# Chunked attention and a gated feed-forward layer on one Trainium2 core: GpSimd's sums of weights handed out seven in five steps instead of two a step

## The chip, the core and the metric

The kernel runs on one core of one Trainium2 chip. The metric is the device time of the whole program in microseconds (us): the median of several runs.

## The reference

Attention works within chunks of 64 positions (8 batches, 8 heads, 576 positions, 64 values per head), and its output, as 4608 tokens of 512 numbers, goes through a gated layer with 1536 inner columns:

```python
scores = scale * np.matmul(q_c, k_c.transpose(0, 1, 2, 4, 3))      # per chunk of 64
scores = scores - np.max(scores, axis=-1, keepdims=True)
attn = np.exp(scores)
attn = attn / (np.sum(attn, axis=-1, keepdims=True) + 1e-09)
out = np.matmul(attn, v_c)
x = out.transpose(0, 2, 1, 3).reshape(B * S, H * D)                # 4608 x 512
gate = 1.0 / (1.0 + np.exp(-(x @ w_gate)))                          # 512 x 1536
val = x @ w_val
return gate * val @ w_out                                           # 1536 x 512
```

## The kernel before

The tokens are nine blocks m of 512. Weights come in twelve groups f of 128 inner columns. All matmul operands are split into a high and a low part, and three products of the parts make one exact enough product (`up`, line 253; `down`, line 281).

**Blocks 0 to 2** run one step per group f: `step(m, f)` (line 602) issues the gate and value products g (12 + 12 matmuls, line 261), ScalarE's sigmoid (`hf`, line 270), VectorE's gating (line 272) and the split into `hh` (ScalarE, line 274) and `hl` (VectorE, line 276); `finish()` then adds the output products of the step before to the four accumulators `acc` (line 287). So "step (2,1)" means block 2, group 1, and the output products of (1,11) stand behind the g products of (2,0). The first two steps of block 1 run earlier; `rest()` (line 645) begins with step (1,2). At the last group, `evacuate` (line 294) copies the four accumulators, even ones on VectorE (line 307), odd ones on ScalarE (line 305), into `ob` and sends them out (line 308).

**Blocks 3 to 8** run in three pairs with a scheme that needs seven products in place of eight, for which it needs sums and differences of weights. These are made once, during blocks 1 and 2, and kept in DRAM: there are 24 **units** (6 pairs of groups, gate or value, 2 halves). `keep_sums` (line 331) makes one unit: on GpSimd (POOL in the profile) two additions of weights into `a_val` (line 338), four 128x128 additions and subtractions into `a_sum` (line 344), and the split into `a_both` (lines 346 and 347); then SyncE issues one 512 KB store of it to `sums` (line 348). `a_val` and `a_sum` take the two buffers of the tag "ob", which `evacuate` of blocks 0 and 1 uses for `ob` too; `a_both` has one buffer. `keep_given` and `keep_outer` copy other weights to DRAM and need no engine but SyncE's queue.

**Attention** of the later blocks is worked in between: `flow()` (line 506) gives pieces. A piece S has the score products `sc` of two units of heads (line 170) and asks for the next queries and keys (`load`, line 144: `qt`, `kbd`, two buffers each); a piece A has the value products `av` (line 231) and asks for the next values (`load_values`, line 155: `vt`). The rest of it is VectorE and ScalarE work that `tick` deals out.

**What sets the order.** On TensorE from the stage `MIDDLE` on, and on VectorE in `rest()`, instructions stand in the order in which the code issues them. ScalarE, GpSimd and SyncE are put in order by the framework's scheduler. Buffers are handed round in the order of the code: an `ob` of block 1 asked for after twenty units has to wait for the twentieth unit's reads. All transfers are issued from one queue, SyncE's (SP, SPq in the profile), and its instructions go one after the other: a transfer that has to wait for data holds every transfer behind it.

`keep(n)` (line 637) takes up to n units from the list; `rest()` calls `keep(2)` behind each step and its `finish()` (line 661).

Of the kernel before, what the change touches and what calls it, by code (L numbers as in the profile page):

```python
# [48 lines left out]
def chunk_attn_moe(ctx: ExitStack, tc: tile.TileContext, q, k, v, w, out):  # L49
# [270 lines left out]
    def keep_given(p, which):  # L320

        t = given[p, which] = dp.tile([P, 3, 2, 256], F32, name=f"given{p}{which}")
        for n, (f, k) in enumerate(((2 * p, 0), (2 * p, 1), (2 * p + 1, 1))):
            nc.sync.dma_start(t[:, n], wt[f, which][:, :, k * 256:(k + 1) * 256].bitcast(F32))

    def keep_outer(f):
        if f % 2 == 0:
            outer[f // 2] = dp.tile([P, 2, 1024], F32, name=f"outer{f // 2}")
        nc.sync.dma_start(outer[f // 2][:, f % 2], wt[f, 2].rearrange("p a n -> p (a n)").bitcast(F32))

    def keep_sums(p, which, c):

        if c == 0:
            sums[p, which] = dp.tile([P, 4, 2, 256], F32, name=f"sums{p}{which}")
        val = mp.tile([P, 4, P], F32, tag="ob", name="a_val")
        for n in range(2):
            parts = wt[2 * p + n, which].rearrange("p a (k c n) -> p a k c n", k=2, c=2)[:, :, :, c].bitcast(F32)
            nc.gpsimd.tensor_tensor(out=val[:, 2 * n:2 * n + 2], in0=parts[:, 0], in1=parts[:, 1], op=ALU.add)  # L338
        sm4 = mp.tile([P, 4, P], F32, tag="ob", name="a_sum")
        for o, x, y, op in (  # L340
            (sm4[:, 1], val[:, 2], val[:, 3], ALU.add), (sm4[:, 0], sm4[:, 1], val[:, 0], ALU.subtract),
            (sm4[:, 2], val[:, 0], val[:, 2], ALU.subtract), (sm4[:, 3], val[:, 1], sm4[:, 0], ALU.subtract),
        ):
            nc.gpsimd.tensor_tensor(out=o, in0=x, in1=y, op=op)  # L344
        both = wp.tile([P, 4, 2, P], F32R, tag="spare", name="a_both")
        nc.gpsimd.tensor_copy(both[:, :, 0], sm4)  # L346
        nc.gpsimd.tensor_tensor(out=both[:, :, 1], in0=sm4, in1=both[:, :, 0].bitcast(F32), op=ALU.subtract)  # L347
        nc.sync.dma_start(
            sums[p, which][:, :, c], both.rearrange("p s a n -> p s (a n)").bitcast(F32))
# [10 lines left out]
    def load_group(n, p, which):  # L360

        one, two = place(2048), place(1536)
        for t, g, s in ((one, 2, slice(0, 2)), (two, 1, slice(2, 4))):
            g0 = 0 if g == 2 else 2
            nc.sync.dma_start(
                t[:, :g * 512].rearrange("p (g n) -> p g n", g=g).bitcast(F32),
                given[p, which][:, g0:g0 + g].rearrange("p g a n -> p g (a n)"))
            nc.sync.dma_start(
                t[:, g * 512:].rearrange("p (s n) -> p s n", s=2).bitcast(F32),
                sums[p, which][:, s].rearrange("p s c n -> p s (c n)"))  # L370
        def of_given(t, n):
            return lambda a, c: t[:, n * 512 + a * 256 + c * P:n * 512 + a * 256 + (c + 1) * P]
        def of_sums(t, n):
            return lambda a, c: t[:, n * 512 + c * 256 + a * P:n * 512 + c * 256 + (a + 1) * P]
        groups[n, p, which] = {
            1: (of_given(one, 0), "B11"), 2: (of_given(one, 1), "B21"), 6: (of_sums(one, 2), "T2"),
            5: (of_sums(one, 3), "T1"), 4: (of_given(two, 0), "T4"), 7: (of_sums(two, 1), "T3"),
            3: (of_sums(two, 2), "B22")}
# [47 lines left out]
    def sole(n, p, which):  # L426
        z = ps_g.tile([P, TB], F32, tag=f"g{which}", name="cz", bufs=1)
        product(n, p, which, 5, z, True, True)
        return z
# [143 lines left out]
    def tick(share):  # L573
        now["ticks"] += 1
        now["credit"] += share
        while now["item"] is not None:
            if isinstance(now["item"], float):
                if now["credit"] < now["item"] / 2:
                    return
                now["credit"] -= now["item"]  # L580
            elif not (now["item"] == "wait" and now["ticks"] > now["since"] + 1
                      or now["item"][0] == "open" and now["item"][1] <= now["open"]):
                break
            advance()
        now["credit"] = min(now["credit"], share)

    def insert(upto=4 * NB, pieces=0):


        if now["item"] == "S" or (  # L590
                now["item"] == "A" and now["unit"] < upto and now["ticks"] >= now["since"] + pieces):
            advance()

    def due(n):

        while now["item"] is not None and len([x for x in xc if x[0] == n]) < 7:
            advance()
# [4 lines left out]
    def step(m, f, span):  # L602
        pending.append(hidden(m, f, spans[span]))

    def finish():
        down(*pending.pop(0))
# [27 lines left out]
        run(op)  # L634
    kept = [(p, which, c) for p in range(6) for which in range(2) for c in range(2)]

    def keep(n):
        for _ in range(n):
            if kept:
                p, which, c = kept.pop(0)  # L640
                if c == 0:
                    keep_given(p, which)
                keep_sums(p, which, c)

    def rest():
        for m in range(1, FIRST_PAIR):
            upto = 4 * (m + 2) if m == 1 else 4 * (m + 3)
            for f in range(2 if m == 1 else 0, NF):
                if m == 2 and f == 7:
                    now["open"] = 0  # L650
                step(m, f, "")
                tick(SHARES[m])
                insert(upto, 2)
                finish()
                tick(SHARES[m])
                insert(upto, 2)
                if m == 1:
                    keep_outer(f)
                    if f == 11:
                        keep_outer(0), keep_outer(1)  # L660
                keep(2)
                if m == 2:
                    if f == 8:
                        for which in range(2):
                            load_group(0, 0, which)
        for n in range(3):
            m0 = FIRST_PAIR + 2 * n
            upto = 4 * (m0 + 4)
            order = [(p, which) for p in range(6) for which in range(2)]
            due(n)  # L670
            for i, (p, which) in enumerate(order):
                if i + 1 < len(order) and i > 0:
                    load_group(n, *order[i + 1])
                if pending:
                    banks[n, "z"] = sole(n, p, which)
                    while pending:
                        finish()
                first(n, p, which)
                tick(SHARES["up"])
                if i:  # L680
                    last(n, *order[i - 1])
                    tick(SHARES["up"] if i < 11 else 0)
                    insert(upto, 1)
                middle(n, p, which)
                tick(SHARES["up"] if i < 11 else 0)
                insert(upto, 1)
            load_outer(0), load_outer(1)
            parts = split(n, 0, 0)
            last(n, *order[-1])
            now["open"] = n + 1  # L690
            for b in range(2):
                for f in range(NF):
                    if f % 2 == 0:
                        later = 6 * b + f // 2 + 2
                        if later < 12:
                            load_outer(later % 6)
                        elif n + 1 < 3:
                            load_group(n + 1, 0, later - 12)
                    hh, hl = parts if f == 0 else split(n, f, b)
                    if (b, f) != (0, 0):  # L700
                        tick(SHARES["down"])
                    if (b, f) == (0, NF - 1):
                        parts = split(n, 0, 1)
                    if (n, b) == (2, 1) and f >= NF - 2:
                        pending.append((f, hh, hl))
                        continue
                    for t in range(4):
                        outward(m0 + b, f, t, hh, hl)
                    insert(upto, 1)

        for i, tiles in ((0, (0, 1, 2)), (1, (0,)), (0, (3,)), (1, (1, 2, 3))):
            f, hh, hl = pending[i]
            for t in tiles:
                outward(NB - 1, f, t, hh, hl)
# [34 lines left out]
```

## Time and profile before

| | |
|---|---|
| median of 3 runs | 956.03 us (954.69 to 957.15) |
| the profiled execution, its own time | 960.18 us |
| its span in the trace | 958.4 us |
| mean granted TensorE clock | 0.989 of full speed |
| TensorE (PE) busy | 929.6 us, 97% of the span |
| VectorE (DVE) busy | 601.8 us, 63% |
| ScalarE (ACT) busy | 340.7 us, 36% |
| GpSimd (POOL) busy | 134.1 us, 14% |

Busy times are shares of the whole span; what a stretch is limited by has to be read in that stretch. A matmul's end in the trace is modelled, so starts are the safer numbers. In square brackets behind a row of a timeline stands how long the engine had been idle before it, and what ended that.

### The profile page before, as it was taken

What the parts mean: (1) busy time and instruction counts of PE and PEld (TensorE: products, weight loads), DVE (VectorE), ACT (ScalarE), POOL (GpSimd) and SP (SyncE); (2) the same over time, 40 slices, a digit from 0 to 9 for tenths busy, and PEclk for the clock granted to TensorE, in tenths of its full rate; (3) what the DMA queues carried; (4) which work ended last, traced back from release to release, by engine and by line L of the source; (5) the groups of instructions that cost most, each with busy time, mean ns of one, the idle gap of its engine ahead of it and who ended that gap; (6) DMA issues with size and microseconds to landing.
All of it is one profiled execution on the core that took longest, in us unless ns stands there. A gap on an engine that the chain in (4) does not pass through costs nothing.

```text
span 958.4 us, 13077 instructions
## 1 busy us (share of the span) xinstructions
PE 929.6 (97%) x4960; PEld 763.5 (80%) x4960; DVE 601.8 (63%) x999; ACT 340.7 (36%) x556; POOL 134.1 (14%) x204
## 2 busy tenths in 40 slices
PE   6999999999969999999999999999999999999998
PEld 4777888888847888788888888888888888888886
DVE  6889973676527657777677675677776635544432
ACT  5799752233214323231333432313143321112222
POOL 1000006999838000000000000000000000000000
PEclk7999999999989999999999999999999999999999
DMA  8688985444453343657666756666565655556661
GB/s 270 215 287 299 307 309 180 132 133 129 136 164 109 102 132 132 193 198 226 207 212 239 252 198 218 228 202 206 179 231 191 218 211 192 196 188 209 220 220 44
DMA packets 81279, 189.61 MB, mean 198 GB/s; under 512 B 7488, under 2 KB 38208, under 8 KB 76608
## 3 DMA queue, kind: packets, MB, share of 16 engines
q1 hardware_dynamic: 81216, 188.77, 58.9%
q8 instruction: 39, 0.64, 0.3%
q14 instruction: 24, 0.20, 0.1%
HBM read 150.99 MB, written 37.75 MB: 197 GB/s over the span
## 4 chain that ended last, share of the span: by engine, by line
PE 70%; POOL 9%; DMA 8%; DVE 5%; ACT 4%; issue 2%; SPq 1%; ACTq 0%; DVEq 0%; POOLq 0%
PE acc L499 21%; PE cy L421 15%; PE cz L421 10%; PE cx L421 10%; PE g L261 6%; PE acc L287 4%; DMA w_raw<-w_in 3%; POOL a_sum L344 3%; POOL a_both L347 3%; DMA sums<-a_both 2%; POOL a_val L338 2%; PE sc L170 2%; PE av L231 2%; POOL a_both L346 1%; DMA out<-ob 1%
## 5 line engine op out<-in xcount | busy, mean ns | idle before, releaser
L261 PE MATMUL g<-xt,w 128*128 128x512 f32 (+1 forms) x960 | 208.7, 372 | 6.0 <-ACT hf L270 1.7
L261 PEld LDWEIGHTS g<-xt,w 128*128 128x128 f32 x960 | 168.1, 189 | 41.5 <-ACT hf L270 4.0
L499 PE MATMUL acc<-wr,hh 128*128 128x512 f32 x576 | 177.7, 390 | 0.0
L421 PE MATMUL cy<-xc,wr 128*128 128x512 f32 x648 | 159.4, 389 | 0.4 <-DVE u L458 0.4
L421 PEld LDWEIGHTS cy<-xc,wr 128*128 128x128 f32 x648 | 121.6, 188 | 26.0 <-DVE u L458 0.8
L499 PEld LDWEIGHTS acc<-wr,hh 128*128 128x128 f32 x576 | 107.9, 188 | 22.7 <-ACT raw L242 0.3
L499 PE MATMUL acc<-wr,hl 128*128 128x512 f32 x288 | 112.0, 389 | 0.0
L421 PE MATMUL cz<-xc,wr 128*128 128x512 f32 x432 | 106.3, 391 | 0.0
L421 PE MATMUL cx<-xc,wr 128*128 128x512 f32 x432 | 106.2, 391 | 0.0
L563 DVE STREAM_TRANSPOSE pbd<-pr 32x256 f32<-32x256 f32 x224 | 97.7, 436 | 4.1
L491 DVE TENSOR_TENSOR hl<-hid,hh 128x512 fp32r<-128x512 f32 x72 | 49.6, 688 | 79.0 <-ACT hh L489 75.8
L421 PEld LDWEIGHTS cz<-xc,wr 128*128 128x128 f32 x432 | 80.6, 188 | 17.6 <-issue 1.2
L421 PEld LDWEIGHTS cx<-xc,wr 128*128 128x128 f32 x432 | 80.7, 188 | 17.4 <-issue 0.9
L287 PE MATMUL acc<-w,hh 128*128 128x512 f32 x288 | 90.6, 396 | 1.1 <-ACT hh L274 0.7
L489 ACT CAST hh<-hid 128x512 fp32r<-128x512 f32 x72 | 44.8, 623 | 123.7 <-PE acc L499 96.3
L287 PEld LDWEIGHTS acc<-w,hh 128*128 128x128 f32 x288 | 52.6, 188 | 13.8 <-issue 1.9
L499 PEld LDWEIGHTS acc<-wr,hl 128*128 128x128 f32 x288 | 54.1, 188 | 11.3
L272 DVE TENSOR_TENSOR hf<-g,hf 128x512 f32<-128x512 f32 (+1 forms) x40 | 25.4, 635 | 57.8 <-PE g L261 53.8
L439 DVE TENSOR_TENSOR u<-cy,s 128x512 f32<-128x512 f32 x36 | 24.8, 688 | 57.9 <-PE cy L421 57.8
L338 POOL TENSOR_TENSOR a_val<-w 128x256 f32<-128x256 f32 x48 | 37.7, 805 | 163.8 <-ACT xt L249 147.4
L458 DVE TENSOR_TENSOR u<-cy,s 128x512 f32<-128x512 f32 x36 | 24.9, 690 | 53.9 <-PE cy L421 53.8
L287 PE MATMUL acc<-w,hl 128*128 128x512 f32 x144 | 56.1, 390 | 0.0
(103 smaller groups left out, 1006.5 us busy)
## 6 DMA issues: line engine op xcount, KB each, us to landing
wr<-sums SPq DMA_DIRECT2D x72, 512.0 KB, 4.5
wr<-outer SPq DMA_DIRECT2D x36, 1024.0 KB, 4.8
w_raw<-w_in SPq DMA_DIRECT2D x36, 512.0 KB, 5.8
wr<-given SPq DMA_DIRECT2D x36, 512.0 KB, 3.6
sums<-a_both SPq DMA_DIRECT2D x24, 512.0 KB, 3.5
qt<-q_in SPq DMA_DIRECT2D x36, 256.0 KB, 4.4
kbd<-k_in SPq DMA_DIRECT2D x72, 128.0 KB, 4.4
vt<-v_in SPq DMA_DIRECT2D x36, 256.0 KB, 4.1
```

Source lines behind the costliest of these rows:

```text
L261: nc.tensor.matmul(ps[:, tok], lhsT=wt[f, which][:, wpart, c:c + P], rhs=x[:, part, i, tok], start=n == 0, stop=n == 11)
L272: nc.vector.tensor_tensor(out=hf, in0=pv, in1=hf, op=ALU.mult)
L287: nc.tensor.matmul(acc[m, t], lhsT=hx[:, ts], rhs=wt[f, 2][:, wpart], start=f == 0 and i == 0, stop=f == NF - 1 and i == 2,)
L338: nc.gpsimd.tensor_tensor(out=val[:, 2 * n:2 * n + 2], in0=parts[:, 0], in1=parts[:, 1], op=ALU.add)
L344: nc.gpsimd.tensor_tensor(out=o, in0=x, in1=y, op=op)
L347: nc.gpsimd.tensor_tensor(out=both[:, :, 1], in0=sm4, in1=both[:, :, 0].bitcast(F32), op=ALU.subtract)
L421: nc.tensor.matmul(bank, lhsT=lhs(wpart, c), rhs=x[:, part, c], start=start and k == 0, stop=stop and k == 5, skip_group_check=True)
L458: nc.vector.tensor_tensor(out=u3, in0=y, in1=s1, op=ALU.add)
L489: nc.scalar.copy(hh, h)
L491: nc.vector.tensor_tensor(out=hl, in0=h, in1=hh.bitcast(F32), op=ALU.subtract)
L499: nc.tensor.matmul(acc[m, t], lhsT=hx[:, ts], rhs=wo[f][:, wpart], start=f == 0 and i == 0, stop=f == NF - 1 and i == 2)
L563: nc.vector.transpose(out=pb[dst, :, c, h, i, :], in_=ps[src, h::2, k, :])
```

## The change

`keep` no longer takes a fixed number but fills up to a total: behind step (m, f) of `rest()` the units handed out so far are to be the whole part of 7·(12m + f − 13)/5.

```diff
-    def keep(n):
-        for _ in range(n):
+    def keep(done, wanted):
+        for _ in range(wanted - done):
             if kept:
                 p, which, c = kept.pop(0)
                 if c == 0:
...
-                keep(2)
+
+                keep(24 - len(kept), (7 * (12 * m + f - 13)) // 5)
```

Counted out, with the total behind each step:

| step | (1,2) | (1,3) | (1,4) | (1,5) | (1,6) | (1,7) | (1,8) | (1,9) | (1,10) | (1,11) | (2,0) | (2,1) | (2,2) to (2,7) |
|---|---|---|---|---|---|---|---|---|---|---|---|---|---|
| before | 2 | 4 | 6 | 8 | 10 | 12 | 14 | 16 | 18 | 20 | 22 | 24 | 24 |
| changed | 1 | 2 | 4 | 5 | 7 | 8 | 9 | 11 | 12 | 14 | 15 | 16 | 18, 19, 21, 22, 23, 24 |

The evacuation of block 1 is issued by the `finish()` of step (2,0), ahead of that step's `keep`: behind 20 units before, behind 14 in the changed kernel.

The instructions of TensorE and of VectorE stand in the same order in both kernels. Three places of SyncE's queue show what moves.

**SyncE's queue ahead of block 1's four outputs** (`sums` the units' stores, `qt` and `kbd` queries and keys for a piece S, `vt` values for a piece A, `out` the evacuation). Before:

```order
L348 DMA sums_2428<-a_both 512x1x256 x2
L348 DMA sums_2537<-a_both 512x1x256
L158 DMA vt<-v_in 128x512 x2
L348 DMA sums_2537<-a_both 512x1x256
L348 DMA sums_2627<-a_both 512x1x256 x2
L149 DMA qt<-q_in 128x512
L152 DMA kbd_87<-k_in 64x2x256 x2
L149 DMA qt<-q_in 128x512
L152 DMA kbd_88<-k_in 64x2x256 x2
L158 DMA vt<-v_in 128x512 x2
L308 DMA out<-ob 128x512 x4
```

Changed:

```order
L348 DMA sums_2540<-a_both 512x1x256 x2
L149 DMA qt<-q_in 128x512
L152 DMA kbd_87<-k_in 64x2x256 x2
L149 DMA qt<-q_in 128x512
L152 DMA kbd_88<-k_in 64x2x256 x2
L158 DMA vt<-v_in 128x512 x2
L149 DMA qt<-q_in 128x512
L152 DMA kbd_87<-k_in 64x2x256 x2
L149 DMA qt<-q_in 128x512
L152 DMA kbd_88<-k_in 64x2x256 x2
L158 DMA vt<-v_in 128x512 x2
L308 DMA out<-ob 128x512 x4
```

The six stores of units 15 to 20 are gone from here. The queries and keys that stand last ahead of the outputs now have no store between them and the queries and keys before them.

**SyncE's queue behind those outputs**, up to the first load of weights for the paired blocks (`wr`). Before:

```order
L348 DMA sums_2752<-a_both 512x1x256
L152 DMA kbd_88<-k_in 64x2x256
L348 DMA sums_2869<-a_both 512x1x256 x2
L158 DMA vt<-v_in 128x512 x2
L149 DMA qt<-q_in 128x512
L152 DMA kbd_87<-k_in 64x2x256 x2
L149 DMA qt<-q_in 128x512
L152 DMA kbd_88<-k_in 64x2x256 x2
L158 DMA vt<-v_in 128x512 x2
L365 DMA wr<-given_1914 128x1024
```

Changed:

```order
L348 DMA sums_2831<-a_both 512x1x256 x2
L158 DMA vt<-v_in 128x512 x2
L348 DMA sums_2942<-a_both 512x1x256 x2
L149 DMA qt<-q_in 128x512
L152 DMA kbd_87<-k_in 64x2x256 x2
L149 DMA qt<-q_in 128x512
L152 DMA kbd_88<-k_in 64x2x256 x2
L348 DMA sums_3055<-a_both 512x1x256 x2
L348 DMA sums_3215<-a_both 512x1x256 x2
L158 DMA vt<-v_in 128x512 x2
L365 DMA wr<-given_1972 128x1024
```

Ten stores stand behind the outputs in place of four. Ahead of the rows shown, unit 15's store now stands ahead of the first keys behind the outputs, as unit 21's did before; the queries and keys shown wait behind unit 20's, and the last values shown behind unit 24's.

**SyncE's queue while the last weights are loaded** (`w_raw` from the input, `given` and `outer` copies of converted weights to DRAM, with the buffers' numbers). Before:

```order
L324 DMA given30_2312<-w_824 128x2x256
L108 DMA w_raw_1198<-w_in 128x1024
L324 DMA given30_2312<-w_824 128x2x256
L324 DMA given30_2312<-w_837 128x2x256
L329 DMA outer4_2310<-w_1180 128x1024
L324 DMA given31_2424<-w_824 128x2x256 x2
L324 DMA given31_2424<-w_837 128x2x256
L329 DMA outer5_2531<-w_1189 128x1024
L108 DMA w_raw_1317<-w_in 128x1024
```

Changed:

```order
L329 DMA outer4_2252<-w_1180 128x1024
L108 DMA w_raw_1198<-w_in 128x1024
L329 DMA outer5_2461<-w_1189 128x1024
L329 DMA outer0_2533<-w_240 128x1024
L329 DMA outer0_2533<-w_397 128x1024
L324 DMA given30_2536<-w_824 128x2x256 x2
L108 DMA w_raw_1317<-w_in 128x1024
```

The copies to DRAM are mixed anew among the loads of weights; one 512 KB copy (`outer4_2252<-w_1180`) now goes ahead of `w_raw_1198` in place of one of 256 KB. On ScalarE, one CAST of a weight moves behind a sigmoid at the same time of the program.

## Rows read from the trace of the kernel before

**Rows 1.** The page, busy tenths in 40 slices of 24 us: TensorE and GpSimd
```profile
PE   6999999999969999999999999999999999999998
...
POOL 1000006999838000000000000000000000000000
```

**Rows 2.** TensorE's timeline: start us, us, line, products, [idle before <-releaser]
```profile
263.49 5.60 PE L261 MATMUL g<-xt,w 128*128 128x512 f32 x24
277.19 1.97 PE L170 MATMUL sc<-kbd,qt 128*64 128x128 f32 x16 [8.10 <-DMA kbd<-k_in]
...
290.06 3.06 PE L261 MATMUL g<-xt,w 128*128 128x512 f32 x12 [1.30 <-DVE hf L272]
...
306.36 5.60 PE L261 MATMUL g<-xt,w 128*128 128x512 f32 x24
```

**Rows 3.** SyncE's queue, timeline around the evacuation of block 1
```profile
258.30 12.81 SPq L348 DMA_DIRECT2D sums<-a_both  x3
271.20 0.58 SPq L149 DMA_DIRECT2D qt<-q_in  x1
...
276.53 7.59 SPq L308 DMA_DIRECT2D out<-ob  x4
```

**Rows 4.** GpSimd's timeline: first unit, end of the 14th, of the 20th, start of the 21st
```profile
152.05 1.45 POOL L338 TENSOR_TENSOR a_val<-w 128x256 f32<-128x256 f32 x2 [147.36 <-ACT xt L249]
...
233.75 1.29 POOL L347 TENSOR_TENSOR a_both<-a_sum,a_both 128x512 fp32r<-128x512 f32 x1
...
269.31 1.26 POOL L347 TENSOR_TENSOR a_both<-a_sum,a_both 128x512 fp32r<-128x512 f32 x1
285.46 1.96 POOL L338 TENSOR_TENSOR a_val<-w 128x256 f32<-128x256 f32 x2 [14.89 <-DMA out<-ob]
```

**Rows 5.** VectorE's timeline: the two evacuation copies of block 1 and step (2,1)'s gating
```profile
267.25 0.69 DVE L307 COPY ob<-acc 128x512 f32<-128x512 f32 x1 [5.70 <-POOL a_sum L344]
282.55 0.69 DVE L307 COPY ob<-acc 128x512 f32<-128x512 f32 x1 [14.62 <-DMA out<-ob]
...
289.31 0.69 DVE L272 TENSOR_TENSOR hf<-g,hf 128x512 f32<-128x512 f32 x1
```

**Rows 6.** Stretches: length, busy PE PEld DVE ACT POOL (instructions), PE clock, DMA share, GB/s
```profile
277.00:281.00 4.00, 3.47 (x30) 3.13 (x32) 0.00 (x0) 0.00 (x0) 0.00 (x0) 0.50 0.84 235
...
230.00:255.00 25.00, 25.00 (x157) 20.75 (x157) 15.74 (x29) 5.80 (x9) 23.58 (x36) 1.00 0.44 143
...
96.00:130.00 34.00, 33.82 (x171) 27.20 (x170) 30.22 (x53) 22.15 (x39) 0.00 (x0) 1.00 0.92 314
```

**Rows 7.** The chain that ended last, pieces of block 2: start us, us, what
```profile
313.86 2.94 PE acc L287 x12
...
322.24 2.72 PE acc L287 x12
324.96 5.44 PE g L261 x24
330.40 1.90 PE av L231 x32
...
340.68 1.90 PE sc L170 x32
...
359.12 1.90 PE av L231 x32
```

**Rows 8.** Outputs and keys: one piece of the chain, and median us from issue to landing
```profile
276.53 5.90 DMA out<-ob
...
kbd<-k_in SPq DMA_DIRECT2D x72, 128.0 KB, 4.4
...
out<-ob SPq DMA_DIRECT2D x24, 256.0 KB, 2.2
```

**Rows 9.** VectorE's split hl, groups by form: 155 to 270 us, then 310 to 380 us
```profile
L276 DVE TENSOR_TENSOR hl<-hf,hh 128x512 fp32r<-128x512 f32 x11 | 10.2, 926 | 7.6 <-ACT hh L274 7.6
...
L276 DVE TENSOR_TENSOR hl<-hf,hh 128x512 fp32r<-128x512 f32 x8 | 5.5, 692 | 5.5 <-ACT hh L274 5.5
```

## The prediction

> **What bounds the kernel now.** I read the page's busy slices first. TensorE is at 9 tenths or more nearly everywhere; behind the first slice there is one low digit, the 6 of the twelfth slice (264 to 288 us), and that is where GpSimd falls from 8 to 3 [rows 1]. Next comes TensorE's timeline across that slice: step (2,1)'s g products start at 263.49, and the score products behind them start only at 277.19, after 8.10 us of idle that the keys' transfer ended. A second, smaller wait of 1.30 us stands ahead of the value products at 290.06, ended by VectorE's gating [rows 2].
>
> SyncE's queue tells why the keys were late. From 258.30 on it spends 12.81 us on three stores, each waiting for its unit; the queries and keys stand behind them and go out from 271.20 on, the outputs of block 1 from 276.53 [rows 3]. GpSimd tells why the stores were late: it works from 152.05 without a real pause, and its 20th unit ends at 269.31 + 1.26 = 270.57 [rows 4]. That is 118.5 us for 20 units, **5.93 us a unit**, more than two units in the 10 us or so that a step takes. VectorE lies in the same stop: its first evacuation copy waited 5.70 us for a buffer of GpSimd's, its second 14.62 us for an output to land, and the gating of step (2,1) follows only at 289.31 [rows 5]. So at this one place a queue of units, not TensorE, sets the pace; elsewhere TensorE does.
>
> **What the stop costs.** From the start of step (2,1) to the start of step (2,4) the trace has 306.36 − 263.49 = 42.87 us [rows 2]. The work between is three steps' g products, one S piece with 12 output products behind it, 12 output products, one A piece with 12 behind it. Undisturbed, further on in block 2, these take 3 × 5.44 + 1.90 + 2.94 + 2.72 + 1.90 + 2.94 = 28.72 us [rows 7]. The difference is **14.15 us**. By these rows 8.10 + 1.30 us of it is idle; part of the rest is the clock: in 277 to 281 us, behind the idle stretch, the granted clock is 0.50, the 1.2 GHz level, against 1.00 or 2.4 GHz before [rows 6], so the score products there took twice their time.
>
> **The change, part by part.**
>
> *Six units less ahead of block 1's evacuation.* Unit 14 ended at 233.75 + 1.29 = 235.04 [rows 4], and nothing ahead of it moves. The buffers are then free well before the first evacuation copy, which without its wait would start at 267.25 − 5.70 = 261.55 [rows 5]. In the queue, the queries and keys for the S piece have no store left ahead of them that is not done by 235; they wait only for the S piece before them, two steps earlier, and land about 4.4 us behind their issue [rows 8], long before 268.9. The 8.10 us go.
>
> *What is late next there.* Only two `ob` buffers serve four copies, so the third and fourth wait for an output to land. Landing takes between 2.2 (median) and 5.90 us [rows 8]. First copy done at 262.24, landed at 264.5 to 268.2, VectorE's second copy done at 265.2 to 268.9. In the trace the gating of (2,1) started 289.31 − 282.55 = 6.76 us behind the start of that second copy [rows 5]; so it would end at 272.0 to 275.7. TensorE wants it at 263.49 + 5.44 + 1.90 + 2.94 + 2.72 = 276.5, for the value products of (2,2). It fits by 0.8 to 4.5 us, so I cost it at nothing; if the cover is gone it costs what it overruns, and I keep 0.5 us for that.
>
> *Ten units behind the evacuation in place of four.* GpSimd now pauses from 235 until the last outputs have landed, at 267.4 to 275 (the second copies' end plus 2.2 to 5.9, and some tenths to issue), and needs 10 × 5.93 = 59.3 us from there, to 327 to 334. Every store holds the queue, so what stands behind stores has to meet TensorE's new dates, 14.15 us earlier than now. Queries and keys behind unit 15: unit done by 281, issue 5.3 us (271.20 to 276.53 for such a set with values behind it [rows 3]), landing 4.4, so 291 against an S piece at 306.36 + 5.44 − 14.15 = 297.7. Queries and keys behind unit 20: 275 + 35.6 + 5.3 + 4.4 = 320.3 against 340.68 − 14.15 = 326.5. Values behind unit 24, two of the eight transfers of such a set (1.3 us): 334 + 1.3 + 4.4 = 340 against 359.12 − 14.15 = 345.0 [rows 7]. All three are met with 5 us or more, at the late end. Weights of the paired blocks, read from DRAM, stand behind them and are used only behind block 2's last step. I cost this part at nothing.
>
> *GpSimd beside VectorE for longer.* Six units now run in block 2. Beside GpSimd, VectorE's split took 926 ns, without it 692 [rows 9]: 0.23 us more. In 230 to 255 us, with GpSimd busy 23.58 us, TensorE was still busy all 25.00 [rows 6], so I take 0, and as bounds 0 and one split per step, 6 × 0.23 = 1.4 us. The Trainium skill speaks against the change here: "SBUF — State Buffer", Who interferes with whom, says that a VectorE instruction with two SBUF inputs and a GpSimd instruction that reads SBUF block each other, the second waiting out the first. The two rows on the split agree with that; whether it reaches TensorE is the first rival below.
>
> *Copies to DRAM mixed anew, one CAST moved.* In 96 to 130 us TensorE is busy 33.82 of 34.00 us and DMA moves 314 GB/s [rows 6]. One transfer 256 KB larger ahead of a weight load is 0.26 MB / 314 GB/s = 0.8 us, if the conversion waits for it. The gain can't exceed the 0.2 us of idle there. I take 0 and keep −0.2 to +0.8.
>
> *The sum.* 960.18 − 14.15 = 946.0 us for the profiled execution. The median of the runs shown is 956.03, 4.15 us below that execution; the same difference gives **941.9 us**. The bounds of the parts (+0.5, +1.4, +0.8, −0.2) and the spread of the runs before, over 1 us to either side, give the forecast its own range of 939.5 to 945.5.
>
> **The rivals.**
>
> *GpSimd and VectorE block each other on TensorE's path.* For it: the split is slower beside GpSimd. Against it: TensorE lost nothing in block 1 under the same load. The worst is one wait as long as a GpSimd instruction, 1.29 us [rows 4], in each of six steps: 7.7 us, 949.6; half of that 945.8. The same interval covers the case that the runs without a profile held a smaller stop (their 4.15 us less might all be from it): a gain of 10.0, 946.0. Chance 0.12.
>
> *The change does nothing that lasts:* TensorE gets past 269 earlier and stops for another reason before 306, say for outputs that land as late as the 5.90 us and a full queue behind them. For it: two buffers for four copies still tie VectorE to the outputs. Against it: the dates above, and that the queue in front of the outputs is empty by then. The gain is then under 3 us: 953 to 959, say 956. Chance 0.05.
>
> *Slower: the stop moves to block 2 and grows.* The place is the values behind unit 24's store. They are late if ten units end after about 339, that is at a pace over 6.4 us (GpSimd starting at 275) or 7.2 us (at 267.4). To be slower than now by over 0.3% the wait must eat 14.15 + 2.9 = 17 us, so unit 24 would end at 356, a pace of 8.1 to 8.9 us. For it: VectorE's work in block 2 also holds the seven operands' differences, with two inputs from SBUF. Against it: 20 units ran at 5.93 beside a VectorE busy 15.74 of 25 us [rows 6]. It gives about 960. Chance 0.04.
>
> **How the numbers follow.** Forecast 0.79, rivals 0.12, 0.05 and 0.04. The range starts at 939.0 and reaches into the first rival, to 948.0; that leaves out the last two and half of the first. A difference of 0.3% (2.9 us) is about what a measurement can tell from none here. Faster by more: the forecast and the first rival, 0.91; within: 0.05; slower: 0.04.
>
> **What would show it.** In the changed profile TensorE's slices have no 6 behind the first; score products follow step (2,1) without idle, at a granted clock of 1.00; the first evacuation copy of block 1 starts near 261.6 without waiting for GpSimd; GpSimd pauses from about 235 to about 270 and works until 327 to 334; and step (2,4) starts 28.7 us behind step (2,1). I am wrong if TensorE waits over 1 us for keys, values or the gating in 265 to 350, or if loads of weights hold it before 150.

## The result, and the profile after

The changed kernel takes **944.93 us** (median of 6 runs, 943.06 to 946.24) against 956.59 us for the kernel before (6 runs, 954.69 to 958.22): a ratio of 0.9877, 95% interval 0.986 to 0.9895, so 11.7 us faster. Timed again beside the experiments on one chip it took 943.18 against 956.47, 0.9857 (0.9835 to 0.9878), so 13.3 us. The forecast was 941.9, with a range of 939.0 to 948.0. The profiled execution took 944.83 us, span 943.0, against 960.18 and 958.4.

The page of the changed kernel, busy tenths of TensorE and GpSimd; the slices are now 23.6 us:

```profile
PE   5999999999999999999999999999999999999998
...
POOL 1000005998069700000000000000000000000000
```

The 6 in TensorE's twelfth slice [rows 1] is gone, and GpSimd has its pause in the eleventh and twelfth instead. TensorE's timeline of the changed kernel across the place:

```profile
262.74 5.60 PE L261 MATMUL g<-xt,w 128*128 128x512 f32 x24
268.27 1.97 PE L170 MATMUL sc<-kbd,qt 128*64 128x128 f32 x32
...
273.02 5.60 PE L261 MATMUL g<-xt,w 128*128 128x512 f32 x24
...
291.46 5.60 PE L261 MATMUL g<-xt,w 128*128 128x512 f32 x24
```

Step (2,1) starts at 262.74, step (2,4) at 291.46: 28.72 us where there were 42.87 [rows 2], with no idle time in brackets. From 265 to 420 us the trace lists one wait of TensorE, of 0.39 us, past the last step of block 2:

```profile
378.01 1.66 PE L421 MATMUL cy<-xc,wr 128*128 128x512 f32 x6 [0.39 <-DVE u L458]
```

The busy times of that stretch and a little beyond, and of 277 to 281 us (length, busy PE PEld DVE ACT POOL, PE clock, DMA share, GB/s):

```profile
262.74:301.74 39.00, 39.00 (x242) 31.98 (x240) 28.90 (x49) 13.45 (x17) 32.87 (x48) 1.00 0.41 136
277.00:281.00 4.00, 4.00 (x20) 3.30 (x19) 3.22 (x7) 0.65 (x2) 3.84 (x6) 1.00 0.53 171
```

The granted clock in 277 to 281 is 1.00, 2.4 GHz, where it was 0.50, 1.2 GHz [rows 6]; TensorE had no idle stretch before it this time.

The other three engines at the place. VectorE, first and second evacuation copy and the gating of (2,1):

```profile
260.94 0.69 DVE L307 COPY ob<-acc 128x512 f32<-128x512 f32 x1 [0.70 <-PE acc L287]
264.25 0.69 DVE L307 COPY ob<-acc 128x512 f32<-128x512 f32 x1 [2.62 <-DMA out<-ob]
...
271.02 0.69 DVE L272 TENSOR_TENSOR hf<-g,hf 128x512 f32<-128x512 f32 x1
```

SyncE's queue, from the last three stores ahead of the outputs to the outputs:

```profile
222.69 11.66 SPq L348 DMA_DIRECT2D sums<-a_both  x3
...
243.41 0.33 SPq L149 DMA_DIRECT2D qt<-q_in  x1
...
261.66 4.18 SPq L308 DMA_DIRECT2D out<-ob  x4
```

GpSimd: end of the 14th unit, start of the 15th, end of the 24th:

```profile
232.51 1.29 POOL L347 TENSOR_TENSOR a_both<-a_sum,a_both 128x512 fp32r<-128x512 f32 x1
267.15 1.95 POOL L338 TENSOR_TENSOR a_val<-w 128x256 f32<-128x256 f32 x2 [33.35 <-DMA out<-ob]
...
325.77 1.27 POOL L347 TENSOR_TENSOR a_both<-a_sum,a_both 128x512 fp32r<-128x512 f32 x1
```

Against [rows 3 to 5]: the first copy waits for TensorE alone, the second 2.62 us for an output to land instead of 14.62; the outputs go out at 261.66 instead of 276.53; GpSimd stands still for 33.35 us without anyone waiting for it, and ends at 327.04 instead of 309.61.

### The profile page after: what moved, and what is told of

Same layout as the page of the kernel before. It is cut to its first block, busy times and chain, and to the rows that moved or that the text cites. A ratio compares the mean times of both kernels' runs of the same rounds, so it can differ in the third digit from the quotient of the medians.

```text
span 943.0 us, 13084 instructions
## 1 busy us (share of the span) xinstructions
PE 925.9 (98%) x4960; PEld 762.5 (81%) x4960; DVE 601.1 (64%) x999; ACT 340.7 (36%) x556; POOL 134.8 (14%) x204
## 4 chain that ended last, share of the span: by engine, by line
PE 86%; DMA 4%; DVE 4%; ACT 4%; issue 1%; SPq 0%; ACTq 0%; DVEq 0%
PE acc L499 21%; PE cy L421 15%; PE g L261 15%; PE cz L421 11%; PE cx L421 10%; PE acc L287 8%; PE sc L170 3%; PE av L231 3%; DMA w_raw<-w_in 3%; ACT w_raw L130 1%; DVE w_raw L132 1%; ACT w_raw L129 1%; DVE w L137 1%; ACT w L136 1%; DVE w_raw L134 1%
## 5 line engine op out<-in xcount | busy, mean ns | idle before, releaser
L287 PEld LDWEIGHTS acc<-w,hh 128*128 128x128 f32 x288 | 52.7, 188 | 13.3 <-issue 1.7
```

The costliest lines, as they stand in the source:

```text
L287: nc.tensor.matmul(acc[m, t], lhsT=hx[:, ts], rhs=wt[f, 2][:, wpart], start=f == 0 and i == 0, stop=f == NF - 1 and i == 2,)
```

## The experiments

In all of them the stop is read as before: from the start of step (2,1) to that of step (2,4), less the undisturbed 28.72 us. Each ratio is against the kernel before, timed on the same chip: 958.22 us for the kernel before again and for 14, 18 and 22 ahead; 956.47 for the changed kernel again, the keys from ScalarE, and ten and four ahead; 957.88 for the stores from GpSimd and the slower start.

**The kernel before, again** (no edit).

> The kernel before once more, unchanged, for a second profile and more times. In its profile on record the stretch from the start of step (2,1) to the start of step (2,4) took 42.87 us against 28.72 undisturbed, a stop of 14.15 us; but that execution's own time, 960.18 us, lies above all six runs (954.69 to 958.22), while the changed kernel's profiled execution, 944.83, lies at its median. Theory A: the stop's length varies between executions by about 3 us; then this profile's stop is shorter the nearer its own time is to 956.6, about 10.5 to 12 us there. Rival: the stop is 14 us in every execution and the 3 us lie elsewhere in the span (start or end); then the stretch is again 42.5 to 43.2 us, whatever the execution's own time.

Measured: 958.85 against 958.22 us, ratio 1.0004 (0.999 to 1.0018); the profiled execution took 959.27. TensorE's timeline, and VectorE's second evacuation copy:

```profile
264.03 5.60 PE L261 MATMUL g<-xt,w 128*128 128x512 f32 x24
277.54 1.98 PE L170 MATMUL sc<-kbd,qt 128*64 128x128 f32 x16 [7.91 <-DMA kbd<-k_in]
...
305.44 5.60 PE L261 MATMUL g<-xt,w 128*128 128x512 f32 x24
```
```profile
281.62 0.69 DVE L307 COPY ob<-acc 128x512 f32<-128x512 f32 x1 [13.18 <-DMA out<-ob]
```

The stop is 305.44 − 264.03 − 28.72 = 12.69 us, 1.5 less than in the first profile, in an execution that took only 0.9 less. So the stop does differ between executions, by 1.5 us here, but not in step with the time of the whole as theory A had it; two profiles can say no more than that. The stretch is 41.41 us, outside the rival's 42.5 to 43.2. Neither expectation holds as written.

**The changed kernel, again** (no edit).

> The changed kernel once more, for a second profile and more times on the same chip as the others. Theory: step (2,1) to step (2,4) takes 28.7 us in every execution, TensorE idles nowhere between 265 and 350, and the times lie at 943 to 946, as before; against the kernel before on the same chip the gain is 11 to 12.5 us. Rival: the gain is the 14 to 15 us that the two profiled executions differ by; then the ratio is 0.984 to 0.986.

Measured: 943.18 us, ratio 0.9857. Step (2,1) to step (2,4) takes 28.72 us again. The gain of 13.3 us is above the 11 to 12.5 that I expected, and the ratio inside what the rival gave; its interval, 0.9835 to 0.9878, reaches into both.

**Two a step, but 14 ahead of the evacuation.**

```diff
-                keep(24 - len(kept), (7 * (12 * m + f - 13)) // 5)
+                keep(24 - len(kept), min(2 * (12 * m + f - 13), 14 if m == 1 else 24))
```

> Two units a step as before, but no more than 14 ahead of block 1's evacuation; the other ten follow two a step behind it. Theory: only the number of units ahead of the evacuation counts, since GpSimd works them off without a pause whatever the pace at which they are handed out; the time is that of the changed kernel, 944.9, within 1 us, and step (2,1) to step (2,4) takes 28.7 us. Rival: the pace of seven in five steps is what helps, by spreading stores and keys; then half the gain or more is lost, 950 to 957.

Measured: 944.46 us, ratio 0.9853 (0.9834 to 0.9871); step (2,1) starts at 262.47, step (2,4) at 291.19, 28.72 us apart. By the edit's formula the ten others are not handed out two a step, as the expectation says: the total jumps from 14 to 22 at step (2,0) and reaches 24 at (2,1). So the pace differs even more from seven in five steps, and the time is the same: the pace is worth nothing by itself, the number ahead of the evacuation is.

**The same with 18 ahead** (18 in place of 14 in that line; the total goes to 22 at step (2,0)).

> As the run with 14 ahead, but 18. Theory: the 18th unit ended at 258.3 us in the kernel before, ahead of the first evacuation copy (261.6 without a wait); the queue is free for the last queries and keys from about 258.3, which land at 267 to 268, just before the score products at 268.9. So nearly all of the gain stays: 945 to 947, and idle ahead of the score products between 0 and 1 us. Rival: the stores ahead of the keys cost in proportion to their number; with 18 instead of 20 ahead only a third of the gain is there, 952 to 954.

Measured: 946.22 us, ratio 0.9876 (0.9856 to 0.9896), as the theory had it. The wait came at another place than I expected: none ahead of the score products, and 0.94 us ahead of the value products, ended by the gating. TensorE:

```profile
261.72 5.60 PE L261 MATMUL g<-xt,w 128*128 128x512 f32 x24
275.82 3.02 PE L261 MATMUL g<-xt,w 128*128 128x512 f32 x12 [0.94 <-DVE hf L272]
...
292.13 5.60 PE L261 MATMUL g<-xt,w 128*128 128x512 f32 x24
```

The stop is 1.69 us. The first copy was on time (259.92 to 260.61), but its output stood behind queries, keys and values in SyncE's queue until 262.80, and the second copy, which waits for it, started only 5.5 us after that (2.6 in the changed kernel, from 261.66 to 264.25). SyncE's queue and VectorE:

```profile
262.80 7.08 SPq L308 DMA_DIRECT2D out<-ob  x4
```
```profile
268.32 0.69 DVE L307 COPY ob<-acc 128x512 f32<-128x512 f32 x1 [7.70 <-DMA out<-ob]
```

**22 ahead.**

```diff
-                keep(24 - len(kept), (7 * (12 * m + f - 13)) // 5)
+                keep(24 - len(kept), min(22, (11 * (12 * m + f - 13) + 4) // 5) if m == 1 else 24)
```

> 22 units ahead of block 1's evacuation in place of 20. Theory: each unit more holds evacuation and keys for another 5.9 us, so GpSimd's 22nd unit ends at about 282.4 and the stop grows by 11 to 12 us: 967 to 969, with step (2,1) to step (2,4) at 54 to 55 us. Rival: the stop is set by something else at this place (landing of outputs, VectorE's order), and two units more change little: 956 to 959.

Measured: 963.5 us, ratio 1.0052 (1.0037 to 1.0067): the right way, but 5 us and not 11. The stop is 309.72 − 262.06 − 28.72 = 18.94 us. GpSimd and VectorE tell why:

```profile
278.39 1.27 POOL L347 TENSOR_TENSOR a_both<-a_sum,a_both 128x512 fp32r<-128x512 f32 x1
```
```profile
285.92 0.69 DVE L307 COPY ob<-acc 128x512 f32<-128x512 f32 x1 [9.67 <-DMA out<-ob]
```

The last unit ahead ends at 279.66, 9.1 us later than the 20th did, but the second copy starts only 3.4 us later. In the kernel before, two sets of queries and keys and the values stood between that unit's store and the outputs, 5.3 us of issuing [rows 3]; here the queries and keys stand ahead of the last two stores, and the outputs go out at 282.01, 2.3 us behind the unit. So they go out 5.5 us later than in the kernel before, and the second copy starts 3.9 us behind them instead of 6.0.

**Queries and keys from ScalarE's queue** (20 ahead, as before).

```diff
-        nc.sync.dma_start(qt, q[g, u].rearrange("p (a n) -> p a n", a=2))
+        issue = nc.scalar if j >= 10 else nc.sync
+        issue.dma_start(qt, q[g, u].rearrange("p (a n) -> p a n", a=2))
...
-            nc.sync.dma_start(kb[s, :, i, :], k[g, u, s].rearrange("p (a n) -> p a n", a=2))
+            issue.dma_start(kb[s, :, i, :], k[g, u, s].rearrange("p (a n) -> p a n", a=2))
```

> The kernel before, twenty units ahead, with the queries and keys from the tenth unit of heads on issued from ScalarE's queue in place of SyncE's; all else stays, the two shared buffers too. Theory: the stop has two parts, keys behind stores in one queue and evacuation copies that wait for GpSimd's buffers. The first is taken away, so the 8 us of idle ahead of the score products go, but the evacuation still starts at 267 and the gating of step (2,1) still ends only at 282 to 286; step (2,1) to step (2,4) takes 35 to 38 us, and the time is 949 to 952. Rival 1: the keys alone were the stop; then the time is that of the changed kernel, 944 to 946. Rival 2: the buffers alone set it and the keys were late beside them; then nothing changes, 955 to 958.

Measured: 956.42 us, ratio 0.9996 (0.9982 to 1.001). That is what rival 2 gave, but by chance and not for its reason: from step (2,1) at 273.82 to step (2,4) at 302.54 it is 28.72 us, no stop at all. The time was lost before. ScalarE's and TensorE's timelines in block 1 (this kernel's lines stand one further down, so L271 is the sigmoid and L262 the g products):

```profile
231.50 0.60 ACT L271 ACTIVATE hf<-g 128x512 f32<-128x512 f32 x1 [16.77 <-DMA sums<-a_both]
```
```profile
232.15 8.01 PE L262 MATMUL g<-xt,w 128*128 128x512 f32 x24 [5.88 <-ACT hf L271]
```

ScalarE stood 16.77 us with its transfers ahead of its sigmoid. The profile names a unit's store as what ended that; why ScalarE's transfers wait for one was not looked into. TensorE, some 10 us late by step (2,1), wanted the evacuation only after GpSimd had ended the 20th unit, at 268.21. This run could not part the two halves of the stop.

**The stores from GpSimd** (20 ahead).

```diff
-        nc.sync.dma_start(
+        nc.gpsimd.dma_start(
             sums[p, which][:, :, c], both.rearrange("p s a n -> p s (a n)").bitcast(F32))
```

> The kernel before, twenty units ahead, with the 24 stores of the units issued by GpSimd itself in place of SyncE's queue, so that no queries, keys, values or outputs stand behind a unit; the shared buffers stay. The run with keys on ScalarE's queue did not part the two halves of the stop, because ScalarE stood still behind its own transfers (16.77 us at the longest) and TensorE lost its time before 263. Theory: the keys are on time, so the idle ahead of the score products goes; the evacuation still waits for the twentieth unit (267 to 271, later by whatever an issue costs GpSimd), but its outputs go out at once and land in 2.2 to 5.9 us, so that the gating of step (2,1) ends at 278 to 281 where TensorE wants it at 276.5. Step (2,1) to step (2,4) then takes 30 to 35 us in place of 41 to 43, and the time is 946 to 952. Rival: the buffers alone make the stop; then 40 us or more stay, and 955 to 958. If an issue costs GpSimd over 0.5 us, all dates of units move by 10 us or more and the stop grows instead.

Measured: 963.53 us, ratio 1.0069 (1.0051 to 1.0088). An issue occupies GpSimd 0.73 us and comes 0.40 us behind the instruction before it, so a unit takes 6.71 us and the 20th ends at 284.58: the last case of the expectation. But the halves are parted now. TensorE, then VectorE's and ScalarE's copies:

```profile
261.75 5.60 PE L261 MATMUL g<-xt,w 128*128 128x512 f32 x24
267.28 1.97 PE L170 MATMUL sc<-kbd,qt 128*64 128x128 f32 x32
282.50 1.22 PE L287 MATMUL acc<-w,hh 128*128 128x512 f32 x2 [13.26 <-DVE ob L307]
...
310.32 5.60 PE L261 MATMUL g<-xt,w 128*128 128x512 f32 x24
```
```profile
281.76 0.69 DVE L307 COPY ob<-acc 128x512 f32<-128x512 f32 x1 [22.46 <-POOL a_sum L344]
284.62 0.69 DVE L307 COPY ob<-acc 128x512 f32<-128x512 f32 x1 [2.17 <-DMA out<-ob]
```
```profile
287.41 0.59 ACT L305 COPY ob<-acc 128x512 f32<-128x512 f32 x1 [2.22 <-DMA out<-ob]
```

The score products come without a wait, and TensorE then waits 13.26 us for the first evacuation copy. The stop is 19.85 us. The buffers alone are enough to stop it, keys or no keys, but at a 20th unit that ends 14.0 us later than in the kernel before (284.58 against 270.57). At the kernel before's dates they would cost less, by an estimate from these rows: 14.0 us less for the unit and 1.7 less because step (2,1) starts at 261.75 here and at 263.49 there, which leaves about 4 us of its 14.15. The rest would then go with SyncE's queue: the second copy starts 2.86 us behind the first here, and 15.30 behind it in the kernel before [rows 5].

**Ten ahead, 14 behind.**

```diff
-                keep(24 - len(kept), (7 * (12 * m + f - 13)) // 5)
+                keep(24 - len(kept), (12 * m + f - 13) if m == 1 else 10 + 2 * (f + 1))
```

> One unit a step in block 1, ten ahead of the evacuation, then two a step: 14 units behind it. GpSimd starts again at about 267 and ends its 24th unit at about 351. In the queue's order for this kernel the values wanted at 345 stand behind unit 21 (333), the queries and keys wanted at 326.5 behind unit 18 (315), and the evacuation of block 2, which takes the shared buffers next, comes at about 366. Theory (dates): all are met, so the time is the changed kernel's, 943.5 to 946. Rival (the slower case of the prediction): fourteen stores in block 2 hold values or keys and TensorE waits 5 us or more there, 949 to 955.

Measured: 944.35 us, ratio 0.9867 (0.9844 to 0.989), as the theory had it. The 24th unit ends at 352.36. Values and keys are on time; the first wait that the ten late units cause is a small one at the start of the paired blocks, for a load of sums:

```profile
364.91 2.57 PE L421 MATMUL cz<-xc,wr 128*128 128x512 f32 x6 [2.60 <-DMA wr<-sums]
```

**Four ahead, 20 behind.**

```diff
-                keep(24 - len(kept), (7 * (12 * m + f - 13)) // 5)
+                keep(24 - len(kept), min(4, f - 1) if m == 1 else 4 + 5 * (f + 1) // 2)
```

> Only four units ahead of block 1's evacuation, twenty behind it. GpSimd starts again at about 267 and needs 20 x 5.9 = 118 us, to about 386. Theory: the same stop comes at the next place where the shared buffers are wanted, block 2's evacuation at about 366: its copies wait for GpSimd, TensorE waits for accumulators, and the weights and the queries behind the last stores are late as well; 15 to 25 us over the changed kernel, 960 to 970, with TensorE's idle time between 366 and 395. Rival: block 2 has other places for half of its outputs and the pairs start with other banks, so that the wait is hidden; then 945 to 950.

Measured: 973.23 us, ratio 1.0178 (1.0152 to 1.0203), 3 us beyond the 960 to 970 that I gave, and 30 us over the changed kernel on the same chip (943.18). TensorE's waits (us in all, times, longest), and three of GpSimd's units:

```profile
PE cz L421 <- DMA wr<-sums: 11.8, 1, 11.8
PE cx L421 <- DVE ob L307: 8.9, 1, 8.9
```
```profile
353.96 2.15 POOL L347 TENSOR_TENSOR a_both<-a_sum,a_both 128x512 fp32r<-128x512 f32 x1
363.48 2.16 POOL L347 TENSOR_TENSOR a_both<-a_sum,a_both 128x512 fp32r<-128x512 f32 x1
372.96 2.12 POOL L347 TENSOR_TENSOR a_both<-a_sum,a_both 128x512 fp32r<-128x512 f32 x1
```

Two waits: weights for the paired blocks, whose sums were not yet stored, and the copies of block 2 for the same buffers as in block 1. Together they are 20.7 us. The granted clock is lower there as well (0.58 to 0.79 in the stretches between 366 and 420 us, against 1.00 in the changed kernel); the rest of the 30 us was not taken apart. These three units come 9.5 us apart, not 5.9; over all twenty, from 270.38 to 398.83, it is 6.4. In 340 to 380 us VectorE makes the seven operands' differences, in groups by form; below it the same group of the kernel before in 310 to 380 us, where GpSimd is done:

```profile
L411 DVE TENSOR_TENSOR xc<-raw,xc 128x1024 fp32r<-128x1024 f32 x7 | 13.0, 1877 | 0.0
```
```profile
L411 DVE TENSOR_TENSOR xc<-raw,xc 128x1024 fp32r<-128x1024 f32 x6 | 7.3, 1219 | 0.0
```

They take 1877 ns beside GpSimd against 1219 without it, and GpSimd's split 2.15 us beside them instead of 1.29 [rows 4].

**A slower start, 14 ahead.**

```diff
-                keep(24 - len(kept), (7 * (12 * m + f - 13)) // 5)
+                keep(24 - len(kept), max(12 * m + f - 13, 2 * (12 * m + f - 13) - 6))
```

> One unit a step for six steps of block 1, then two: 14 ahead of the evacuation as in the changed kernel, the ten others two a step, so that the last is handed out at step (2,4) in place of (2,7). It asks whether a version is better than the changed kernel: the copies to DRAM among the loads of weights stand as in the run with ten ahead, which began step (1,2) at 156.4 us against 159.5 in the changed kernel. Theory: that lead comes mostly from the first transfers of the program landing sooner in that execution, and the pace behind 14 does not count, so the time is that of the changed kernel, 943 to 945.5. Rival: the order of the copies gives the 2 to 3 us; then 940 to 942.

Measured: 943.55 us, ratio 0.9855 (0.9833 to 0.9877): as the theory had it, no better than the changed kernel. Step (1,2) began at 158.96. No version here beats the changed kernel by more than the runs scatter.

## Why the prediction was right, point by point

**The place and the cause: right.** The number of units ahead of block 1's evacuation sets the stop. With ten, and with 14 at any pace, it is 0, with 18 it is 1.69 us, with 20 it is 12.69 and 14.15, with 22 it is 18.94. The number counts through the date of the last unit: with the keys on ScalarE's queue twenty ahead made no stop, where TensorE came 10 us later and no keys stood ahead of the outputs.

**The cost of the stop: right in the trace.** I forecast 14.15 us and 28.72 us for the stretch. All four profiles with 14 ahead (the changed kernel's, its second one, the run at two a step and the slower start) have 28.72. I named 8.10 + 1.30 us of the stop as idle; three shorter waits, of 0.34, 0.35 and 0.76 us, make it 10.85, and only the other 3.3 us are work done more slowly.

**What holds TensorE: right in its parts, but not in which of them decides.** I wrote first of the queries and keys, whose 8.10 us stood in front. The runs show which chain decides: the second evacuation copy. Its start, counted from the start of step (2,1), goes with the stop:

| run | last unit ahead ends | second copy, from step (2,1) | stop |
|---|---|---|---|
| 14 ahead, changed kernel | 233.80 | 1.51 | 0 |
| 18 ahead | 256.50 | 6.60 | 1.69 |
| 20 ahead, second profile | 271.07 | 17.59 | 12.69 |
| 20 ahead, first profile | 270.57 | 19.06 | 14.15 |
| 22 ahead | 279.66 | 23.86 | 18.94 |

Where there is a stop it is 4.9 us less than the second copy's lag, each time to 0.02 us: what VectorE overruns is what TensorE loses. The wait for keys in the kernel before lay within this one. The keys did harm by standing ahead of the outputs in the queue, as 18 and 22 ahead show, and the stores from GpSimd show the stop with keys on time. In that run VectorE's second copy, at 284.62, lags 22.87 us and ScalarE's, at 287.41, 25.66: there ScalarE's sets it.

That chain is made of both halves. In the kernel before the second copy comes 17.55 us later, from step (2,1), than in the changed one (19.06 against 1.51). Of that, 5.70 us are the first copy's wait for GpSimd's buffer; 8.6 are the time that its output then stood in the queue, from 267.94 to 276.53, behind unit 20's store, the keys and the values [rows 3, 5]; and 3.4 the longer way from there to the second copy, 6.0 us against 2.6. My account put the keys' lateness first and did not price the outputs' place behind them. No run gave the evacuation buffers of its own, which would part the two by measurement.

**What is late next: right.** I had the second copy done at 265.2 to 268.9 and the gating ended at 272.0 to 275.7; it was 264.94 and 271.71, a little ahead of both, since the first copy started 0.6 us sooner and its output landed in some 2.6 us, near the median. TensorE did not wait. By the 4.9 us above, the cover was 3.4 us (4.9 less the lag of 1.51), within my 0.8 to 4.5.

**Ten units behind: right.** Forecast were a restart at 267.4 to 275 and an end at 327 to 334; measured 267.15 and 327.04. The dates for keys and values were met: TensorE has no wait between 265 and 378 us.

**GpSimd beside VectorE: right that it costs nothing.** The split `hl` in 268 to 330 us of the changed kernel takes 974 ns (926 with GpSimd and 692 without in the kernel before [rows 9]):

```profile
L276 DVE TENSOR_TENSOR hl<-hf,hh 128x512 fp32r<-128x512 f32 x7 | 6.8, 974 | 4.8 <-ACT hh L274 4.8
```

TensorE is busy 39.00 of 39.00 us beside it. The rule of the Trainium skill ("SBUF — State Buffer", Who interferes with whom) is seen at work on both engines, and in this kernel's dates it costs nothing; with four units ahead, where three units run beside the operands' differences, those come 9.5 us apart. My slower rival needed 8.1 to 8.9 as the mean of ten units, and even that run has 6.4 over all its units; its waits were for weights and for block 2's buffers, not for the values that I named. In the changed kernel the last unit ends at 327.04, and the first of those differences starts at 346.31.

**Copies to DRAM mixed anew: outside my bounds, small, its cause open.** I kept −0.2 to +0.8 us. Step (2,1) starts 0.75 us earlier in the first pair of profiles (262.74 against 263.49) and 1.53 in the second (262.50 against 264.03). I took 96 to 130 us for the only place where this could count. The lead does not come from there: it is already 1.10 us in the first pair at the g products that start at 90.99 (92.09 in the kernel before) and 2.62 in the second (90.69 against 93.31), and shrinks by step (1,2) to 0.75 (159.50 against 160.25) and 1.53. Whether the copies' order makes it, or executions that differ early on, was not tried. No load of weights held TensorE before 150: its longest wait for weights there is 0.9 us, for a CAST on ScalarE, as in the kernel before.

**From the trace to the median: the step that missed by 3 us.** I carried over the difference between the profiled execution and the median, 4.15 us, as if it were constant. The changed kernel's profiled execution, 944.83, lies at its median, and the kernel before's lay above all six of its first runs. The trace's gain of 15.4 us of span (0.75 ahead of the place, 14.15 at it, 0.5 behind) stands against 11.7 and 13.3 us between medians of the two kernels; the two other versions with 14 ahead gained 13.8 and 14.3 on their chips, near the 14.1 that I forecast, so the first 11.7 is the low end. The stop itself was 1.5 us shorter in the second profile; that is part of it, and the rest stays open. The time alone would not have chosen the mechanism: 944.93 lies nearer to the first rival's 945.8 and 946.0 than to my 941.9. Against that rival's blocking stands the trace, in which TensorE waits for nothing behind the place; its other case, a smaller stop in the runs without a profile, is in part what happened. The lower end of my own range, 939.5, does not come out of its terms either: 941.9 less 0.2 and 1.3 is 940.4.

## What to carry to other kernels

Where one queue issues all transfers, count for each shared buffer how many jobs stand ahead of the next user that matters, and see that the engine that works them off ends the last of them before that user's date; look also at what stands in the queue behind that job's store. In this kernel the pace at which the jobs are handed out did not matter, the number ahead did. Read the stop from the chain that ends last, here the second copy, and not from the wait that is seen first: the visible wait for keys hid a longer one. Moving work behind a date is free only up to the next date: ten ahead is still as good within the scatter of the runs, four costs 30 us (973.23 against 943.18 on the same chip).

## What the runs showed of the hardware

An engine that issues transfers can stand still behind them: ScalarE's sigmoid waited 16.77 us. The Trainium skill ("DMA: Bandwidth & Descriptors", Issuing engines are not separate DMA queues) says that issuing on several engines saves only the issuing time, usually small beside the transfer. Here the measurement differs: with the stores on GpSimd the keys went out at 242.42 instead of 271.20, and the score products' wait of 8 us was gone, because what held the keys was not an issue but the wait of a store ahead of them. It was no gain in time (963.53 us): GpSimd's units took 6.71 us instead of 5.93, and the stop grew.

GpSimd and VectorE slowed each other by more than I took from one split: with four ahead, units of 5.9 us came 9.5 us apart beside VectorE instructions with two inputs of 128x1024, which took 1877 ns instead of 1219.
